# Memory sums joined with a U round, denominators from GpSimd sums, and a halved last tile, in a fused attention and SwiGLU kernel

## The chip, the cores and the metric

One core of one Trainium2 chip. The metric is the device time of one execution in microseconds (us), the median of several; lower is better. A profile is one further execution; its span is about 2 us shorter than the time on the device. Batch numbers run from 0 to 7, and "batch b" also names the part of the program in which batch b's gate and value matmuls run.

## The reference

Cut to what matters:

```python
a = exp(phi - max(phi)); a = a / (sum(a over the 32 memories) + 1e-9)      # (8, 8, 576, 32)
k_m = einsum('bhsm,bhsd->bhmd', a, k);  v_m = einsum('bhsm,bhsd->bhmd', a, v)
scores = q @ k_m.T / 8;  attn = softmax(scores);  x = attn @ v_m           # heads side by side: (4608, 512)
out = (silu(x @ w_gate) * (x @ w_val)) @ w_out                             # 512 -> 1536 -> 512
```

Inputs and output are float32. The kernel multiplies v_m into the two weight matrices first (the "U rounds"), so that gate and value come from the attention weights directly. It divides the memory sums by sums over the tokens ("denominators"), one for each head and memory.

## The kernel before

For each batch it makes memory sums (`kv_sum`: 48 matmuls, each on a strip of 32 array columns, four at a time), denominators (12 full-array matmuls with one moving column), a reciprocal and two normalisations on VectorE, and a transposition. Three U rounds (16 matmuls each, on tiles of 64 rows by 32 columns) and 24 "slots" follow. A slot is a gate pair, its silu on ScalarE, and the value pair and multiply of the slot before. Between the slots lie output matmuls of earlier batches. The whole is one hand-made order.

```python
def kv_denominators(b, p, o):
    for g in range(NG):
        for j in range(J):                                   # 2 x 6 matmuls
            nc.tensor.matmul(p[:, o + g:o + g + 1], lhsT=ephis[b][:, j, g]..., rhs=ones1[0:P, :], ...)
    r = att.tile([128, NG, 1, 1], FP32, tag="rS", name="t_rS")
    nc.vector.reciprocal(out=..., in_=p[:, o:o + NG])        # reads the denominators
# ...
def kv_items(b):
    def sums():
        box["kv"] = ps.tile([128, NG * 2 * D + NG], FP32, tag="b", name="p_kv")   # one PSUM tile for
        kv_sum(b, box["kv"], (0, 1))                                             # sums and denominators
    def norm():
        kv_denominators(b, box["kv"], o); k_norm(...); v_norm(...)
    return [lambda: (sums(), norm()), lambda: kv_T(b, (0, 1))]
# ... in the loop over batches, b = 2..7:
streams = [(g, 0, 24), (rest, 0, 24), ([u_item(b, 2)], 5, 6)]
streams += [([lambda: load_qT(b + 1)], n, n), (kv_items(b + 1), 8, 14),          # sums behind slot 9
            ([u_item(b + 1, 0)], 15, 17), ([u_item(b + 1, 1)], 21, 23)]
```

`spread` merges streams by their positions, counted in slots. PSUM is the memory that the matmuls write to; the pool `ps` has six of its banks, used in turn, and the output tiles have two more. SBUF is the memory that holds all other tiles.

The softmax here doesn't subtract the row's maximum and nothing guards it: scores larger than these inputs give would overflow.

Of the kernel before, what the change touches and what calls it, by code (L numbers as in the profile page):

```python
# [9 lines left out]
FP32 = mybir.dt.float32  # L10
BF16 = mybir.dt.bfloat16
# [3 lines left out]
def kernel(  # L15
# [17 lines left out]
    nc = tc.nc  # L33
    AF = mybir.ActivationFunctionType
    ALU = mybir.AluOpType

    B, H, S, D = q.shape
    M = phi.shape[3]
    DM, DF = moe_w_gate.shape
    P, J = 96, 6  # L40
    NG = 2
# [10 lines left out]
    att = ctx.enter_context(tc.tile_pool(name="att", bufs=2))  # L52
# [3 lines left out]
    ps = ctx.enter_context(tc.tile_pool(name="ps", bufs=6, space=bass.MemoryType.PSUM))  # L56
# [4 lines left out]
    out_r = out.rearrange("(b p j) c -> b j p c", b=B, p=P, j=J)  # L61
# [78 lines left out]
    ephis, rSs, bks, bvs, kTs, es, atts = {}, {}, {}, {}, {}, {}, {}  # L140

    def phi_exp(b):
        t = att.tile([P, J, NG, NP, M], BF16, tag="ephi", name="t_ephi")
        src = phis.pop(b).rearrange("p (i g) (j m) -> p g i j m", g=NG, m=M)
        for g in range(NG):
            nc.scalar.activation(  # L146
                out=t[:, :, g].rearrange("p j i m -> p i j m"), in_=src[:, g], func=AF.Exp
            )
        ephis[b] = t

    box = {}

    def kv_sum(b, p, parts):

        w0, w1 = parts[0], parts[-1] + 1
        n = (w1 - w0) * D
        for g in range(NG):
            for j in range(J):
                for i in range(NP):
                    nc.tensor.matmul(  # L160
                        p[32 * i:32 * i + 32, n * g:n * (g + 1)],
                        lhsT=ephis[b][:, j, g, i],
                        rhs=kvs[b][:, w0:w1, 2 * i + g, j * D:(j + 1) * D],
                        start=(j == 0),
                        stop=(j == J - 1),
                        tile_position=(0, 32 * i),
                    )

    def kv_denominators(b, p, o):
        for g in range(NG):  # L170
            for j in range(J):
                nc.tensor.matmul(  # L172
                    p[:, o + g:o + g + 1],
                    lhsT=ephis[b][:, j, g].rearrange("p i m -> p (i m)"),
                    rhs=ones1[0:P, :],
                    start=(j == 0),
                    stop=(j == J - 1),
                )
        r = att.tile([128, NG, 1, 1], FP32, tag="rS", name="t_rS")
        nc.vector.reciprocal(  # L180
            out=r.rearrange("p g a c -> p (g a c)"), in_=p[:, o:o + NG]
        )
        rSs[b] = r

    def k_norm(b, p):
        bk = att.tile([128, NG, 2, D], BF16, tag="bk", name="t_bk")
        nc.vector.tensor_tensor(
            out=bk,
            in0=p.to_broadcast([128, NG, 2, D]),
            in1=rSs[b].to_broadcast([128, NG, 2, D]),  # L190
            op=ALU.mult,
        )
        bks[b] = bk

    def v_norm(b, p):
        bv = att.tile([128, NG, D], BF16, tag="bv", name="t_bv")
        nc.vector.tensor_tensor(
            out=bv,
            in0=p,
            in1=rSs[b].rearrange("p g a c -> p g (a c)").to_broadcast([128, NG, D]),  # L200
            op=ALU.mult,
        )
        bvs[b] = bv

    def kv_T(b, parts):
        p = ps.tile([128, 3, 128], BF16, tag="b", name="p_T")
        if 0 in parts:
            kTs[b] = att.tile([128, 3, 128], BF16, tag="kT", name="t_kT")
        if 1 in parts:
            nc.tensor.transpose(p[:, 2], bvs.pop(b).rearrange("p g d -> p (g d)"), ident)  # L210
        if 0 in parts:
            bk = bks.pop(b)
            for g in range(NG):
                nc.tensor.transpose(p[:, g], bk[:, g].rearrange("p a d -> p (a d)"), ident)
        lo, hi = (0 if 0 in parts else 2), (3 if 1 in parts else 2)
        nc.vector.tensor_copy(out=kTs[b][:, lo:hi], in_=p[:, lo:hi])  # L216

    def kv_items(b):


        def sums():
            box["kv"] = ps.tile([128, NG * 2 * D + NG], FP32, tag="b", name="p_kv")
            kv_sum(b, box["kv"], (0, 1))

        def norm():
            o = NG * 2 * D
            kv_denominators(b, box["kv"], o)
            kvv = box["kv"][:, 0:o].rearrange("p (g w d) -> p g w d", g=NG, w=2)
            k_norm(b, kvv[:, :, 0:1, :])
            v_norm(b, kvv[:, :, 1, :])  # L230

        return [lambda: (sums(), norm()), lambda: kv_T(b, (0, 1))]

    def k_items(b):

# [118 lines left out]
    def flush_mul():  # L354
        while pend:
            pend.pop(0)()
# [44 lines left out]
    def token_segments(t0, count):  # L401
        segs = []
        t = t0
        while t < t0 + count:
            bb, rest = divmod(t, S)
            blk, pp = divmod(rest, P)
            n = min(P - pp, t0 + count - t)
            segs.append((t - t0, n, bb, 2 * (blk % 3) + blk // 3, pp))
            t += n
        return segs  # L410

    def out_units(c, u, eng):

        mine = {}

        def unit(jf):
            def run():
                if jf == 0:
                    mine["p"] = po.tile([128, DM], FP32, tag="o", name="p_oo")
                nc.tensor.matmul(  # L420
                    mine["p"],
                    lhsT=hts[c, jf][:, 128 * u:128 * (u + 1)],
                    rhs=WO[jf],
                    start=(jf == 0),
                    stop=(jf == NJF - 1),
                )
                if jf == NJF - 1:
                    t_o = work.tile([128, DM], FP32, tag="to", name="t_o")
                    if eng == "a":
                        nc.scalar.copy(out=t_o, in_=mine["p"])  # L430
                    else:
                        nc.vector.tensor_copy(out=t_o, in_=mine["p"])  # L432
                    for (r0, n, bb, jj, pp) in token_segments(2 * c * S + 128 * u, 128):
                        nc.sync.dma_start(
                            out=out_r[bb, jj, pp:pp + n, :], in_=t_o[r0:r0 + n, :]
                        )

            return run

        return [unit(jf) for jf in range(NJF)]  # L440

    def out_list(b):
        tiles = range(0, 4) if b % 2 == 0 else range(4, 9)
        res = []
        for n, u in enumerate(tiles):
            res += out_units(b // 2, u, "v" if n % 4 != 3 else "a")
        return res

    def q_items(b, evac):
# [4 lines left out]
    def u_item(b, c, evac="avav"):  # L454

        both = ((0, c, (0, 1)), (1, c, (0, 1)))
        return lambda: u_round(b, both, evac)
# [9 lines left out]
    def run(items):  # L467
        for x in items:
            x()
# [10 lines left out]
    def exp_tables():  # L480
        nc.scalar.preload_act_table_set("natural_log_exp_and_others")  # L481
# [108 lines left out]
    for b in range(2, B):  # L590
        last = b + 1 == B
        exp_tables()
        if b == 2:
            load_qT(2)
            phi_exp(2)
            run(take(28))
            run(kv_items(2)[:1] + take(6) + kv_items(2)[1:] + take(14))
        run(take(2))
        for g in range(NG):
            scores(b, g)  # L600
        if b + 2 < B:
            load_q(b + 2)
        if not last:
            load_k(b + 1)
            load_v(b + 1)
        if b + 2 < B:
            load_phi(b + 2, nc.gpsimd)
        run(take(8))
        if not last:
            phi_exp(b + 1)  # L610
        for g in range(NG):
            z_inv(b, g)
        nc.scalar.preload_act_table_set("silu_and_others")
        run(take(14))
        norm(b, 0)
        norm(b, 1)
        if b == 2:
            run(take(4))
            run([u_item(2, 0)] + take(6) + [u_item(2, 1)])
        run(take(12))  # L620
        rest = take(len(backlog))
        g = gv_slots(b)
        streams = [(g, 0, 24), (rest, 0, 24), ([u_item(b, 2)], 5, 6)]
        if not last:
            n = 12 if b == 2 else 0
            streams += [
                ([lambda: load_qT(b + 1)], n, n),
                (kv_items(b + 1), 8, 14),
                ([u_item(b + 1, 0)], 15, 17),
                ([u_item(b + 1, 1)], 21, 23),  # L630
            ]
        spread(*streams)
        flush_mul()
        backlog += out_list(b)
# [29 lines left out]
```

## Time and profile before

| | before |
|---|---|
| time, 6 runs in the same rounds as the change | 254.95 us (254.66 to 255.45) |
| span of the profiled run, mean granted TensorE clock | 252.3 us, 0.997 |
| busy: TensorE, VectorE, ScalarE, GpSimd | 243.2, 153.5, 167.0, 36.3 us |
| v of batch 3: issued, landed | 70.96, 87.9 us |
| batch 2: first gate matmul to the next scores | 80.79 to 100.00 us |

TensorE is the engine to watch: it never rests for long after the start, and its granted clock, the row below in tenths of full speed for 40 equal slices of the span, is low in no slice before the last.

```profile
PEclk9999999999999999999999999999999999999998
```

### The profile page before, as it was taken

How to read it: one execution, taken by the hardware profiler on the slowest of the kernel's cores; microseconds unless marked ns; L12 is line 12 of the kernel's file. 1: busy time of each engine (PE TensorE's matmuls, PEld its weight loads, DVE VectorE, ACT ScalarE, POOL GpSimd, SP SyncE). 2: the span in 40 equal slices, each digit the busy share in tenths (PEclk: the TensorE clock that was granted, in tenths of full speed). 3: DMA queues.
4: the chain of work that ended last, by engine and by line, in shares of the span. 5: the costliest groups of instructions: out<-in, count | busy, mean ns of one | idle time of the engine just before them, and what ended most of it. 6: DMA issues, size and time to landing. Idle time of an engine off the chain costs nothing.

```text
span 252.3 us, 6668 instructions
## 1 busy us (share of the span) xinstructions
PE 243.2 (96%) x2642; PEld 148.9 (59%) x2642; DVE 153.5 (61%) x334; ACT 167.0 (66%) x364; POOL 36.3 (14%) x53
## 2 busy tenths in 40 slices
PE   7999799999999999999999999999999999999992
PEld 7976467674544565467645665466645765467541
DVE  0027699993217878377927776487826775587321
ACT  2459689884095758965896578875896668676200
POOL 8433354000140004004000150000000000000000
PEclk9999999999999999999999999999999999999998
DMA  6999999999799998993994599990035211310143
GB/s 184 205 203 201 198 197 203 227 218 150 160 178 244 262 151 125 244 240 42 202 224 107 96 165 238 230 234 5 5 83 136 44 42 44 83 44 0 52 114 83
DMA packets 49006, 36.99 MB, mean 147 GB/s; under 512 B 15952, under 2 KB 43600, under 8 KB 48976
## 3 DMA queue, kind: packets, MB, share of 16 engines
q0 software_dynamic: 27632, 22.42, 55.8%
q1 hardware_dynamic: 20560, 13.57, 22.7%
q10 hardware_dynamic: 784, 0.59, 0.9%
q8 instruction: 20, 0.33, 0.5%
q14 instruction: 10, 0.08, 0.1%
HBM read 42.47 MB, written 9.44 MB: 206 GB/s over the span
## 4 chain that ended last, share of the span: by engine, by line
PE 68%; DMA 27%; POOL 1%; issue 1%; DVE 1%; ACT 0%; POOLq 0%; SPq 0%
PE p_oo L420 29%; PE p_g L364 15%; PE p_v L364 15%; DMA t_kv<-in_v_dram 13%; DMA t_q<-in_q_dram 12%; PE p_u L330 4%; DMA t_qT<-t_q 2%; PE p_kv L160 2%; PE p_kv L172 1%; PE p_g L287 1%; POOL t_kv L74 1%; PE p_v L307 1%; PE p_g L307 1%; POOL t_q L93 0%; POOL t_phi L69 0%
## 5 line engine op out<-in xcount | busy, mean ns | idle before, releaser
L420 PE MATMUL p_oo<-WO,t_h 128*128 128x512 bf16 x432 | 113.1, 379 | 0.0
L380 ACT ACTIVATE t_sg<-p_g 128x288 bf16<-128x288 f32 x192 | 77.2, 415 | 39.6 <-PE p_g L364 33.8
L387 DVE TENSOR_TENSOR t_h<-t_sg,p_v 128x288 bf16<-128x288 bf16 x192 | 84.3, 452 | 22.4 <-PE p_v L364 18.9
L364 PEld LDWEIGHTS <-t_U 128*128 128x128 bf16 x768 | 72.6, 98 | 35.6 <-issue 6.8
L364 PE MATMUL p_g<-t_A,t_U 128*128 128x288 bf16 x384 | 78.5, 286 | 0.8 <-ACT t_U L346 0.8
L364 PE MATMUL p_v<-t_A,t_U 128*128 128x288 bf16 x384 | 77.6, 286 | 0.0
L420 PEld LDWEIGHTS <-t_h 128*128 128x128 bf16 x432 | 41.5, 98 | 40.0 <-issue 2.8
L432 DVE COPY t_o<-p_oo 128x512 f32<-128x512 f32 x28 | 19.3, 691 | 47.2 <-PE p_oo L420 45.0
L348 DVE CAST t_U<-p_u 128x512 bf16<-128x512 f32 (+1 forms) x52 | 31.2, 642 | 1.0 <-PE p_u L330 0.5
L346 ACT CAST t_U<-p_u 128x512 bf16<-128x512 f32 (+1 forms) x52 | 26.2, 556 | 7.1 <-PE p_u L330 6.9
L93 POOL DMA_DIRECT2D t_q<-in_q_dram x6 | 4.6, 774 | 91.7 <-DMA t_qT<-t_q 90.9
L430 ACT COPY t_o<-p_oo 128x512 f32<-128x512 f32 x8 | 4.7, 591 | 19.7 <-PE p_oo L420 10.2
L490 PE MATMUL p_oo<-bones 128*128 128x128 bf16 x218 | 15.9, 234 | 1.5 <-DVE bones L502 1.5
L330 PE MATMUL p_u<-W,t_kT 64*32 64x512 bf16 (+1 forms) x416 | 15.7, 365 | 0.7 <-DVE t_kT L216 0.7
L490 PEld LDWEIGHTS <-bones 128*128 128x128 bf16 x218 | 14.2, 106 | 2.2 <-DVE bones L502 1.5
L146 ACT ACTIVATE t_ephi<-t_phi 96x768 bf16<-96x768 f32 x16 | 12.5, 844 | 4.2 <-DMA t_phi<-in_phi_dram 4.2
L180 DVE RECIPROCAL t_rS<-p_kv 128x2 f32<-128x2 f32 x8 | 1.4, 171 | 18.5 <-PE p_kv L172 18.5
L316 DVE TENSOR_TENSOR t_A<-t_E,t_lz 128x576 bf16<-128x576 bf16 x16 | 11.5, 750 | 0.4 <-ACT t_lz L311 0.4
L311 ACT ACTIVATE t_lz<-t_lz 128x576 f32<-128x576 f32 x16 | 10.9, 683 | 0.5
L481 ACT ACT_TABLE_LOAD x7 | 9.0, 1283 | 1.3 <-PEq L648 1.2
L330 PEld LDWEIGHTS <-t_kT 64*32 64x32 bf16 x416 | 4.3, 89 | 8.3 <-issue 6.6
L160 PE MATMUL p_kv<-t_kv,t_ephi 96*32 96x128 bf16 (+1 forms) x480 | 7.3, 210 | 0.7 <-DMA t_kv<-in_v_dram 0.7
(42 smaller groups left out, 127.8 us busy)
## 6 DMA issues: line engine op xcount, KB each, us to landing
t_kv<-in_k_dram POOLq DMA_DIRECT2D x8, 576.0 KB, 11.0
t_kv<-in_v_dram POOLq DMA_DIRECT2D x8, 576.0 KB, 16.4
out_dram<-t_o SPq DMA_DIRECT2D x24, 192.0 KB, 2.6
t_phi<-in_phi_dram POOLq DMA_DIRECT2D x6, 576.0 KB, 14.5
t_q<-in_q_dram POOLq DMA_DIRECT2D x6, 576.0 KB, 7.4
out_dram<-t_o SPq DMA_DIRECT2D x24, 128.0 KB, 2.4
W<-in_moe_w_gate_dram POOLq DMA_DIRECT2D x6, 256.0 KB, 13.1
W<-in_moe_w_val_dram POOLq DMA_DIRECT2D x6, 256.0 KB, 13.0
```

Source lines behind the costliest of these rows:

```text
L146: nc.scalar.activation(out=t[:, :, g].rearrange("p j i m -> p i j m"), in_=src[:, g], func=AF.Exp)
L160: nc.tensor.matmul(p[32 * i:32 * i + 32, n * g:n * (g + 1)], lhsT=ephis[b][:, j, g, i], rhs=kvs[b][:, w0:w1, 2 * i + g, j * D:(j + 1) * D] ...
L316: nc.vector.tensor_tensor(out=a, in0=es.pop((b, g)), in1=lzs.pop((b, g)), op=ALU.mult)
L330: nc.tensor.matmul(p[g][32 * i:32 * i + 32, f0:f1], lhsT=kTs[b][64 * g:64 * g + 64, 2, 32 * i:32 * i + 32], rhs=W[which, c][64 * g:64 * g ...
L346: nc.scalar.copy(out=t, in_=p)
L348: nc.vector.tensor_copy(out=t, in_=p)
L364: nc.tensor.matmul(p[:, 0:HALF], lhsT=Us[b, which, c, g][:, 128 * o:128 * (o + 1)], rhs=atts[b, g][:, r], start=(g == 0), stop=(g == NG - 1),)
L380: nc.scalar.activation(out=sg, in_=gate, func=AF.Silu)
L387: nc.vector.tensor_tensor(out=dst, in0=sg, in1=val, op=ALU.mult)
L420: nc.tensor.matmul(mine["p"], lhsT=hts[c, jf][:, 128 * u:128 * (u + 1)], rhs=WO[jf], start=(jf == 0), stop=(jf == NJF - 1),)
L432: nc.vector.tensor_copy(out=t_o, in_=mine["p"])
L490: nc.tensor.matmul(p[:, 0:128], lhsT=bones, rhs=bones, start=True, stop=True)
```

## The change

Its intent: fewer small matmuls and fewer changes of TensorE's tiling. GpSimd, nearly idle, adds the six token groups of exp(phi) and splits the sum into two bf16 terms, so 4 instead of 12 matmuls give the denominators. These stand first, then the sums, then a U round right behind them, as one stretch. The stretch has a new place, position 5 to 11 instead of 8 to 14. The very last output tile is copied in two halves by two engines and sent from two queues.

```diff
+    def phi_sum(b):
+        e = ephis[b].rearrange("p j g i m -> p j (g i m)")
+        t = att.tile([P, NG * 128], FP32, tag="es", bufs=1, name="t_es")
+        nc.gpsimd.tensor_tensor(out=t, in0=e[:, 0], in1=e[:, 1], op=ALU.add)
+        for j in range(2, J):
+            nc.gpsimd.tensor_tensor(out=t, in0=t, in1=e[:, j], op=ALU.add)
+        hl = att.tile([P, 2, NG * 128], BF16, tag="ehl", bufs=1, name="t_ehl")
+        nc.gpsimd.tensor_copy(out=hl[:, 0], in_=t)
+        nc.gpsimd.tensor_tensor(out=hl[:, 1], in0=t, in1=hl[:, 0], op=ALU.subtract)
...
+        def run_sums():
+            p = ps.tile([128, o + NG], FP32, tag="b", name="p_kv")
+            kv_denominators(b, p, o)          # ends with the reciprocal, as before
+            kv_sum(b, p, (0, 1))
             k_norm(...); v_norm(...)
+            if beside:
+                beside()                      # the U round
...
+                    if eng == "av":
+                        nc.scalar.copy(out=t_o[:, 0:h], in_=mine["p"][:, 0:h])
+                        nc.vector.tensor_copy(out=t_o[:, h:], in_=mine["p"][:, h:])
...
             phi_exp(b + 1)
+            phi_sum(b + 1)
...
-                (kv_items(b + 1), 8, 14),
+                (kv_items(b + 1, u_item(b, 2)), 5, 11),
```

More of the change, by code (lines that the diff above doesn't have):

```diff
@@ L151 @@
     box = {}
+    esums = {}
+    def phi_sum(b):
[7 more added lines that the diff above has]
+        nc.gpsimd.tensor_tensor(out=hl[:, 1], in0=t, in1=hl[:, 0], op=ALU.subtract)
+        esums[b] = hl
     def kv_sum(b, p, parts):
@@ L169, in kv_denominators, with kv_reciprocal @@
     def kv_denominators(b, p, o):
+        if b in esums:
+            hl = esums.pop(b)
+            terms = [[hl[:, t, 128 * g:128 * (g + 1)] for t in range(2)] for g in range(NG)]
+        else:
+            terms = [
+                [ephis[b][:, j, g].rearrange("p i m -> p (i m)") for j in range(J)]
+                for g in range(NG)
+            ]
         for g in range(NG):
-            for j in range(J):
+            for n, x in enumerate(terms[g]):
                 nc.tensor.matmul(
                     p[:, o + g:o + g + 1],
-                    lhsT=ephis[b][:, j, g].rearrange("p i m -> p (i m)"),
+                    lhsT=x,
                     rhs=ones1[0:P, :],
-                    start=(j == 0),
-                    stop=(j == J - 1),
-                )
+                    start=(n == 0),
+                    stop=(n == len(terms[g]) - 1),
+                )
+        kv_reciprocal(b, p, o)
+    def kv_reciprocal(b, p, o):
         r = att.tile([128, NG, 1, 1], FP32, tag="rS", name="t_rS")
@@ L216, in kv_T, with kv_items @@
         nc.vector.tensor_copy(out=kTs[b][:, lo:hi], in_=p[:, lo:hi])
-    def kv_items(b):
-        def sums():
-            box["kv"] = ps.tile([128, NG * 2 * D + NG], FP32, tag="b", name="p_kv")
-            kv_sum(b, box["kv"], (0, 1))
-        def norm():
+    def kv_items(b, beside=None):
+        def run_sums():
             o = NG * 2 * D
-            kv_denominators(b, box["kv"], o)
-            kvv = box["kv"][:, 0:o].rearrange("p (g w d) -> p g w d", g=NG, w=2)
+            p = ps.tile([128, o + NG], FP32, tag="b", name="p_kv")
+            kv_denominators(b, p, o)
+            kv_sum(b, p, (0, 1))
+            kvv = p[:, 0:o].rearrange("p (g w d) -> p g w d", g=NG, w=2)
             k_norm(b, kvv[:, :, 0:1, :])
             v_norm(b, kvv[:, :, 1, :])
-        return [lambda: (sums(), norm()), lambda: kv_T(b, (0, 1))]
+            if beside:
+                beside()
+        return [run_sums, lambda: kv_T(b, (0, 1))]
     def k_items(b):
@@ L428, in run @@
                     t_o = work.tile([128, DM], FP32, tag="to", name="t_o")
-                    if eng == "a":
+                    if eng == "av":
+                        h = DM // 2
+                        nc.scalar.copy(out=t_o[:, 0:h], in_=mine["p"][:, 0:h])
+                        nc.vector.tensor_copy(out=t_o[:, h:], in_=mine["p"][:, h:])
+                    elif eng == "a":
                         nc.scalar.copy(out=t_o, in_=mine["p"])
@@ L433, in run @@
                     for (r0, n, bb, jj, pp) in token_segments(2 * c * S + 128 * u, 128):
-                        nc.sync.dma_start(
-                            out=out_r[bb, jj, pp:pp + n, :], in_=t_o[r0:r0 + n, :]
-                        )
+                        o_r = out_r[bb, jj, pp:pp + n, :]
+                        if eng == "av":
+                            nc.scalar.dma_start(out=o_r[:, 0:h], in_=t_o[r0:r0 + n, 0:h])
+                            nc.sync.dma_start(out=o_r[:, h:], in_=t_o[r0:r0 + n, h:])
+                        else:
+                            nc.sync.dma_start(out=o_r, in_=t_o[r0:r0 + n, :])
             return run
@@ L445, in out_list @@
         for n, u in enumerate(tiles):
-            res += out_units(b // 2, u, "v" if n % 4 != 3 else "a")
+            eng = "av" if b + 1 == B and u == tiles[-1] else "v" if n % 4 != 3 else "a"
+            res += out_units(b // 2, u, eng)
         return res
@@ L622 @@
         g = gv_slots(b)
-        streams = [(g, 0, 24), (rest, 0, 24), ([u_item(b, 2)], 5, 6)]
+        streams = [(g, 0, 24), (rest, 0, 24)]
+        if last:
+            streams += [([u_item(b, 2)], 5, 6)]
         if not last:
```

## The prediction

> **What bounds the kernel now.** I read the busy shares first, then the chain that ended last, then the timeline of TensorE around one memory sum and one U round, then the waits of TensorE, and the timeline of VectorE before the gate and value rounds.
>
> ```profile
> PE 243.2 (96%) x2642; PEld 148.9 (59%) x2642; DVE 153.5 (61%) x334; ACT 167.0 (66%) x364; POOL 36.3 (14%) x53
> ...
> PE 68%; DMA 27%; POOL 1%; issue 1%; DVE 1%; ACT 0%; POOLq 0%; SPq 0%
> ```
>
> TensorE is busy nearly throughout, and the chain is TensorE work plus 27% DMA. The chain in order of time says where the DMA part lies: before about 88 us. From there to the end it is TensorE, without a break. So after 88 us, time saved on TensorE is time saved, and every stall of TensorE is paid in full; before 88 us loads set the pace. The last load on the chain is v of batch 3:
>
> ```profile
> 69.44 0.67 POOL t_q L93
> 70.20 0.76 POOL t_kv L74
> 70.96 16.95 DMA t_kv<-in_v_dram
> 88.05 0.85 PE p_kv L160 x48
> 88.91 0.39 PE p_kv L172 x12
> ```
>
> The reader is to see that v of batch 3 lands at 70.96 + 16.95 = 87.9 us and that its memory sums start right then. TensorE's timeline of that place (start, length, what) and of a quiet one later:
>
> ```profile
> 83.88 0.41 PE L364 MATMUL p_v<-t_A,t_U 128*128 128x288 bf16 x2
> 84.22 0.63 PE L330 MATMUL p_u<-W,t_kT 64*32 64x512 bf16 x16
> 84.78 0.39 PE L420 MATMUL p_oo<-WO,t_h 128*128 128x512 bf16 x1
> ...
> 87.15 0.41 PE L364 MATMUL p_v<-t_A,t_U 128*128 128x288 bf16 x2
> 88.05 0.85 PE L160 MATMUL p_kv<-t_kv,t_ephi 96*32 96x128 bf16 x48 [0.49 <-DMA t_kv<-in_v_dram]
> ...
> 114.36 0.41 PE L364 MATMUL p_v<-t_A,t_U 128*128 128x288 bf16 x2
> 114.70 0.85 PE L160 MATMUL p_kv<-t_kv,t_ephi 96*32 96x128 bf16 x48
> 115.48 0.45 PE L172 MATMUL p_kv<-ones,t_ephi 96*128 96x1 bf16 x12
> 115.80 0.41 PE L364 MATMUL p_g<-t_A,t_U 128*128 128x288 bf16 x2
> ```
>
> A pair of gate or value matmuls starts every 0.245 us (288 columns each). After the pair at 83.88 the next instruction could start at 84.13; the U round starts at 84.22 and the next full-array matmul at 84.78. A U round therefore costs 0.65 us: single starts in the trace give 0.10 to get in, 0.44 of work (two waves of eight), 0.12 to get out. Memory sums with denominators cost 115.80 - 114.60 = 1.19 us: 0.10 in, 0.68 of sums, 0.10 out, 0.31 for twelve one-column matmuls at about 25 ns.
>
> **What the Trainium skill says.** "TensorEngine Tiling (Array Packing)", Key Properties: a change of tiling mode, not just of tile, drains TensorE. The trace agrees: the 0.10 and 0.12 us on either side of each column-tiled stretch. Sums (96 rows by 32 columns) and U (64 by 32) are by that page's list two modes, so joining them need not make their border free.
> "GPSIMD Engine Reference", section 3.1: an add of two fp32 tensors with 2048 columns took 4497 ns on GpSimd. No run here has such an add yet; scaled to 256 columns plus some dispatch I estimate 0.6 us each.
> "SBUF — State Buffer", Who interferes with whom: a VectorE instruction with two SBUF inputs contends with a GpSimd instruction that reads SBUF, and the later one waits for the whole earlier one. In this kernel only the softmax normalisation (t_A from t_E and t_lz) has two SBUF inputs; before has nothing on GpSimd to meet it, so its trace cannot say.
> "TensorE: Matmul & The Clock Gate", Part 1: an idle window of about 3.4 us halves the clock. Before has no such gap after the start, and its granted clock is 1.00 in every stretch from 62 to 235 us.
>
> **The change, part by part.**
> Denominators, batches 3 to 7: 8 of 12 one-column matmuls go, 8 x 25 ns = 0.20 us each batch. GpSimd gets seven operations per batch, about 4.2 us by the estimate above, in a time in which it is idle.
> Joined stretch, same batches: before 1.19 + 0.65 = 1.84 us. After: four denominators 0.11, in 0.10, sums 0.68, border x, U 0.44, out 0.12 = 1.45 + x. The whole gain is 0.39 - x; with x about 0.1, as for the other mode changes, 0.3 us per batch.
> Moved: the order of TensorE's instructions shows that the sums now stand after gate slot 6 instead of slot 9, three slots earlier, with U2 behind them. In batches 3 to 6 the loads allow it: v of batch 4 is issued at 96.27 and lands 11.3 us later, at 107.6, while the new place is near 111.5. So four batches gain 4 x 0.3 = 1.2 us.
> In batch 2 (sums of batch 3) the load does not allow it. Up to the end of slot 5 nothing changes (84.13 us). Then come one output matmul (0.22), slot 6 (0.49) and the denominators (0.11): TensorE arrives at 84.95 and v lands at 87.9 as before, since nothing ahead of it in the queues changes. It stands about 3.0 us, where before stood 0.5. At 88.05 the new kernel has yet to do what the old had done: U2, slots 7 to 9 (3 x 0.49 = 1.47) and two output matmuls (0.43; order counts four before the stretch where before had six). From there to slot 10 the old kernel needs sums and denominators, 1.09; the new one needs sums 0.68, border 0.1, U 0.44, out 0.12, then 1.47 + 0.43 = 3.24. Loss in batch 2: 2.1 us, its own joining gain already inside.
> Last tile: the copy that ends the kernel is
>
> ```profile
> 247.91 0.69 DVE L432 COPY t_o<-p_oo 128x512 f32<-128x512 f32 x1 [4.49 <-PE p_oo L420]
> ```
>
> Half of it by VectorE takes some 0.42 us (its 256-column casts of U took 417 ns), the ScalarE half about the same (375 ns), side by side. The two transfers of each half are issued from two queues, two per queue as before. Gain 0.27 us.
>
> Sum without contention: 254.82 + 2.1 - 1.2 - 0.3 = 255.4. I add 0.1 for PSUM: the joined stretch takes five of six banks at once, and VectorE must do two normalisations (0.3 and 0.2 us between starts) before its two casts (0.6 each); by my count the banks come free within 0.1 us of when the next slots want them.
>
> **Rivals.**
> GpSimd against the normalisation. In batch 3:
>
> ```profile
> 102.12 1.58 ACT L146 ACTIVATE t_ephi<-t_phi 96x768 bf16<-96x768 f32 x2
> ...
> 106.42 1.42 DVE L316 TENSOR_TENSOR t_A<-t_E,t_lz 128x576 bf16<-128x576 bf16 x2
> ```
>
> GpSimd may start once the exponentials end at 103.7 and works to about 108; VectorE's two normalisations at 106.42 to 107.84 fall inside, and the gate round that reads them starts at 108.21. With up to 0.6 us of waiting before each, they end 0.3 to 1.2 us later, of which about 0.4 is slack: 0 to 0.8 us of stall in each of batches 3 to 6, so 0 to 3 us. For it: the skill and the timing. Against it: it has not been seen here, and if the sums take under 0.4 us each GpSimd is done first. In batch 2 two U rounds lie between, so there is slack. I count 0.4 us for it, a sixth of the worst. If it is whole, the time is about 258.
> The stall cools TensorE. Three us of standing is just short of the 3.4 us window; if it counts, several us at half clock follow and cost 1.5 to 2 us more, 257.5. I give it one in ten.
> The load lands earlier, or the stretch waits for nothing. Then batch 2 gains 0.3 like the others instead of losing 2.1, and the time is 253.2. Against it: before already waited 0.49 us for this very transfer at a place 3 us later. I give it one in eight.
> The border costs nothing (x = 0): 0.5 us better.
> GpSimd as a queue. It also issues the loads, and now cannot run ahead of its sums: k and v of batch 7, issued at 147 us before, must wait for the exponentials of batch 6, about 160. They are needed at 195 and take 10 to 19 us: hidden.
>
> **Range and chances.** 255.4 + 0.1 + 0.4 = 255.9. Eight in ten between 253.8 (v early, or x = 0 with no contention) and 258.3 (full contention, or a cold clock). Two per cent is 5.1 us: no single rival reaches it, and slower needs contention and cooling together. Faster by 2% would need 249.7, more than all savings together.
>
> **What would show it.** Right: a wait of TensorE for v of about 3 us at the first joined stretch, near 85 us, and none at the four later ones; those four stretches, from denominators to the next full-array matmul, at about 1.55 us. GpSimd's sums at 4 us per batch. The normalisations longer or later than 106.4 plus 1.42 would show contention, and then an idle of TensorE before the first gate matmul of the batch. A granted clock under 1.00 after 88 us would show cooling. The last copy at 0.4 us in two engines. Wrong: v landing before 86 us, or TensorE waiting at the stretch for GpSimd's sums instead.

## The result, and the profile after

261.54 us (259.99 to 263.70, 6 runs) against 254.95 us: slower. The ratio is 1.0259, 95% interval 1.0209 to 1.0308. Here and below a ratio is the mean time of one kernel's fast runs over that of the other's fast runs of the same rounds, so it is not quite the ratio of the medians. All six runs count as fast runs, yet their mean granted clocks lie between 0.983 and 0.993. The output is correct.

The busy row and the clock row of the changed kernel's page, and the first row of its chain:

```profile
PE 243.0 (93%) x2575; PEld 150.7 (58%) x2602; DVE 155.9 (60%) x334; ACT 167.5 (64%) x365; POOL 62.4 (24%) x88
...
PEclk9999999999999779999999999999999999999998
...
PE 81%; DMA 8%; DVE 5%; ACT 2%; issue 2%; POOL 0%; DVEq 0%
```

By the page TensorE is busy about as long as before (27 of its 2602 matmuls are missing from this record), so most of the lost 7.9 us of span is not more work. Two slices near 90 us show a low clock, and VectorE, 1% of the chain before, is now 5%. Starts of single instructions give where the time came from. Each row runs from a batch's first gate matmul to the next batch's first score matmul; what lies between these rows takes the same in both kernels, within 0.01 us.

| part | before, us | after, us | difference |
|---|---|---|---|
| start to the first scores of batch 2 | 69.10 | 69.44 | +0.35 |
| batch 2 | 19.21 | 24.56 | +5.35 |
| batch 3 | 18.22 | 18.80 | +0.58 |
| batch 4 | 20.81 | 21.34 | +0.53 |
| batch 5 | 18.22 | 18.61 | +0.39 |
| batch 6 | 20.81 | 21.33 | +0.52 |
| batch 7, to the last matmul's start | 27.75 | 27.75 | 0.00 |
| last matmul's start to the end | 4.84 | 5.02 | +0.19 |

The sum is 7.9 us. Batch 2, the load and the clock: TensorE's timeline, then busy times and clock by stretch (the columns are the stretch and its length; the busy times of TensorE, its weight loads, VectorE, ScalarE and GpSimd, with counts; the clock; the share of DMA and its GB/s).

```profile
85.18 0.24 PE L193 MATMUL p_kv<-ones,t_ehl 96*128 96x1 bf16 x4
88.98 1.47 PE L173 MATMUL p_kv<-t_kv,t_ephi 96*32 96x128 bf16 x48 [3.56 <-DMA t_kv<-in_v_dram]
90.38 1.05 PE L354 MATMUL p_u<-W,t_kT 64*32 64x512 bf16 x16
91.37 0.66 PE L388 MATMUL p_g<-t_A,t_U 128*128 128x288 bf16 x2
```

```profile
84.36:87.77 3.41, 1.07 (x12) 0.73 (x9) 1.34 (x4) 0.82 (x2) 0.00 (x0) 1.00 1.21 281
87.77:91.18 3.41, 2.20 (x64) 1.38 (x64) 0.68 (x3) 0.10 (x1) 0.00 (x0) 0.50 1.15 237
91.18:94.60 3.42, 3.20 (x19) 1.80 (x13) 2.12 (x4) 1.71 (x4) 0.00 (x0) 0.50 0.36 80
94.60:98.01 3.41, 3.41 (x29) 2.62 (x28) 2.26 (x6) 2.21 (x6) 3.09 (x4) 1.00 0.54 52
```

TensorE reaches the stretch at 85.2 and stands until v lands at 88.8. The clock halves at 87.77, while it stands, and is back at 94.60: the sums take 1.40 us to the start of the U round, against 0.78 in every other batch. When the clock steps is seen again under experiment 8.

The later batches: TensorE and VectorE at the joined stretch of batch 4.

```profile
146.32 0.24 PE L193 MATMUL p_kv<-ones,t_ehl 96*128 96x1 bf16 x4
146.96 0.85 PE L173 MATMUL p_kv<-t_kv,t_ephi 96*32 96x128 bf16 x48 [0.40 <-DVE t_rS L204]
147.74 0.63 PE L354 MATMUL p_u<-W,t_kT 64*32 64x512 bf16 x16
148.30 0.42 PE L388 MATMUL p_g<-t_A,t_U 128*128 128x288 bf16 x2
```

```profile
146.37 0.45 DVE L411 TENSOR_TENSOR t_h<-t_sg,p_v 128x288 bf16<-128x288 bf16 x1 [0.25 <-PE p_v L388]
146.75 0.16 DVE L204 RECIPROCAL t_rS<-p_kv 128x2 f32<-128x2 f32 x1
```

This was in none of my steps. The sums wait for the reciprocal, and the reciprocal waits its turn on VectorE behind the multiply of the slot before. Sums and denominators share a PSUM tile; VectorE reads the denominators from it and TensorE then writes the sums to it, and a semaphore holds the sums until the read is over. From first denominator to first sum it takes 0.64 us in batches 4 and 6 and 0.86 in 3 and 5. The joined stretch takes 148.30 - 146.32 = 1.98 us, where sums, denominators and U round took 1.84 apart.

The normalisations of batch 4 on VectorE and, beside them, GpSimd:

```profile
139.46 2.24 DVE L340 TENSOR_TENSOR t_A<-t_E,t_lz 128x576 bf16<-128x576 bf16 x2
```

```profile
137.04 0.66 POOL L158 TENSOR_TENSOR t_es<-t_ephi 96x256 f32<-96x256 bf16 x1 [10.99 <-ACT t_ephi L146]
137.78 3.30 POOL L160 TENSOR_TENSOR t_es<-t_es,t_ephi 96x256 f32<-96x256 f32 x4
141.14 0.81 POOL L162 CAST t_ehl<-t_es 96x256 bf16<-96x256 f32 x1
```

The pair takes 2.24 us where it took 1.42 before, and GpSimd's sums lie around it. The second gate matmul of the batch comes late, 0.51 us after the first instead of 0.12. The end of the kernel, ScalarE and VectorE:

```profile
255.63 0.37 ACT L455 COPY t_o<-p_oo 128x256 f32<-128x256 f32 x1 [2.00 <-DMA out_dram<-t_o]
```

```profile
256.03 0.42 DVE L456 COPY t_o<-p_oo 128x256 f32<-128x256 f32 x1 [4.89 <-ACT t_o L455]
```

The halves do not run side by side: a semaphore holds VectorE until ScalarE has ended, and 0.37 + 0.42 is more than the 0.69 of one copy. The halves share the PSUM tile that they read and the SBUF tile that they write; which of the two the semaphore guards no run separates.

### The profile page after: what moved, and what is told of

Same layout as the page of the kernel before. It is cut to its first block, busy times and chain, and to the rows that moved or that the text cites. A ratio compares the mean times of both kernels' runs of the same rounds, so it can differ in the third digit from the quotient of the medians.

```text
span 260.2 us, 6617 instructions
## 1 busy us (share of the span) xinstructions
PE 243.0 (93%) x2575; PEld 150.7 (58%) x2602; DVE 155.9 (60%) x334; ACT 167.5 (64%) x365; POOL 62.4 (24%) x88
## 4 chain that ended last, share of the span: by engine, by line
PE 81%; DMA 8%; DVE 5%; ACT 2%; issue 2%; POOL 0%; DVEq 0%
PE p_oo L444 27%; PE p_g L388 20%; PE p_v L388 18%; DMA t_kv<-in_v_dram 7%; PE p_u L354 5%; PE p_oo L522 5%; PE p_kv L173 3%; DVE t_A L340 1%; PE p_g L311 1%; DVE t_h L411 1%; DMA out_dram<-t_o 1%; PE p_g L331 1%; DVE t_o L460 1%; PE p_v L331 1%; ACT L593 0%
## 5 line engine op out<-in xcount | busy, mean ns | idle before, releaser
L444 PE MATMUL p_oo<-WO,t_h 128*128 128x512 bf16 x405 | 106.3, 380 | 0.9 <-issue 0.3
L388 PE MATMUL p_g<-t_A,t_U 128*128 128x288 bf16 x384 | 79.7, 289 | 2.6 <-ACT t_U L370 1.0
L460 DVE COPY t_o<-p_oo 128x512 f32<-128x512 f32 x27 | 18.6, 688 | 40.3 <-PE p_oo L444 40.1
L158 POOL TENSOR_TENSOR t_es<-t_ephi 96x256 f32<-96x256 bf16 x5 | 3.3, 663 | 55.3 <-ACT t_ephi L146 55.3
L160 POOL TENSOR_TENSOR t_es<-t_es,t_ephi 96x256 f32<-96x256 f32 x20 | 14.9, 747 | 1.6
L340 DVE TENSOR_TENSOR t_A<-t_E,t_lz 128x576 bf16<-128x576 bf16 x16 | 14.8, 953 | 0.4 <-ACT t_lz L335 0.4
L173 PE MATMUL p_kv<-t_kv,t_ephi 96*32 96x128 bf16 (+1 forms) x480 | 8.0, 219 | 5.8 <-DMA t_kv<-in_v_dram 3.6
L173 PEld LDWEIGHTS <-t_ephi 96*32 96x32 bf16 x480 | 6.9, 101 | 6.9 <-issue 6.5
```

The lines of the kernel that those rows point to most:

```text
L160: nc.gpsimd.tensor_tensor(out=t, in0=t, in1=e[:, j], op=ALU.add)
L173: nc.tensor.matmul(p[32 * i:32 * i + 32, n * g:n * (g + 1)], lhsT=ephis[b][:, j, g, i], rhs=kvs[b][:, w0:w1, 2 * i + g, j * D:(j + 1) * D] ...
L340: nc.vector.tensor_tensor(out=a, in0=es.pop((b, g)), in1=lzs.pop((b, g)), op=ALU.mult)
L388: nc.tensor.matmul(p[:, 0:HALF], lhsT=Us[b, which, c, g][:, 128 * o:128 * (o + 1)], rhs=atts[b, g][:, r], start=(g == 0), stop=(g == NG - 1),)
L444: nc.tensor.matmul(mine["p"], lhsT=hts[c, jf][:, 128 * u:128 * (u + 1)], rhs=WO[jf], start=(jf == 0), stop=(jf == NJF - 1),)
L460: nc.vector.tensor_copy(out=t_o, in_=mine["p"])
```

## The experiments

Ten kernels ran, all with correct results. The first four shared one chip, the next four a second, the last two a third. Each was compared with runs of the kernel before on its own chip, so ratios are compared across the groups, not times. The change itself was not run again beside them; where intervals overlap, the trace has to decide.

**1. The reciprocal behind the sums.**

```diff
             kv_denominators(b, p, o)      # without its reciprocal
             kv_sum(b, p, (0, 1))
+            kv_reciprocal(b, p, o)
```

> The changed kernel with the reciprocal of the denominators issued behind the memory sums instead of ahead of them. Theory (sums and denominators share one PSUM tile, so the sums wait until VectorE has read the denominators, and VectorE comes to that only after its queued multiply): the waits of the sums for the reciprocal (2.3 us in all, 0.4 to 0.65 in each later batch) are gone, batches 3 to 6 lose nothing or gain 0.1 to 0.3 us each, and the time falls from 261.5 by 2.2 to 2.6 us, to about 259.0. Rival (the wait only moves: VectorE's later normalisations hold the five PSUM banks and the next slots wait for those): the waits appear at the gate or value matmuls behind the stretch and the time falls by under 1 us. The first stretch keeps its wait for v and its cold clock under both.

Measured: 259.75 us (258.79 to 261.10, 4 runs), ratio 1.0176 (1.0121 to 1.0231) against the change's 1.0259 (1.0209 to 1.0308). The difference of 0.0083 is 2.1 us of 255; the two intervals overlap, so the size rests on the trace. There, no wait for the reciprocal is left. TensorE at batch 4:

```profile
146.45 0.24 PE L193 MATMUL p_kv<-ones,t_ehl 96*128 96x1 bf16 x4
146.62 0.85 PE L173 MATMUL p_kv<-t_kv,t_ephi 96*32 96x128 bf16 x48
147.41 0.62 PE L355 MATMUL p_u<-W,t_kT 64*32 64x512 bf16 x16
147.96 0.42 PE L389 MATMUL p_g<-t_A,t_U 128*128 128x288 bf16 x2
148.41 0.42 PE L389 MATMUL p_v<-t_A,t_U 128*128 128x288 bf16 x2
```

First denominator to first sum is now 0.17 us in each of batches 3 to 6, where it was 0.86, 0.64, 0.86 and 0.64: 2.3 us saved. The joined stretch takes 147.96 - 146.45 = 1.52 us, 0.33 less than the 1.84 apart, as foreseen. The rival is partly right too. The value pair starts at 148.41, 0.45 us after the gate pair instead of 0.245: by the order of the pool it takes the bank of the sums, and it starts 0.06 us after VectorE has read that bank for the last time (148.35). That gives back 0.2 us in batch 4. Batches 3 to 6 differ from before by -0.03, +0.26, -0.22 and +0.26 us: that none of them would lose was a miss, since the late normalisations, experiment 4, are still in.

**2. The first joined stretch back at its old place.**

```diff
-                (kv_items(b + 1, u_item(b, 2)), 5, 11),
+                (kv_items(b + 1, u_item(b, 2)), *((8, 14) if b == 2 else (5, 11))),
```

> The changed kernel with the joined stretch of batch 2 alone back at its old place (after gate slot 9), all else as changed. Theory (the early place costs the wait for v and, through it, the clock): the granted clock is 1.00 throughout after the start, the wait for v shrinks to under 1 us, and the time falls from 261.5 by 4.5 to 5.3 us, to about 256.5. Rival (only the wait counts; the low clock is a coincidence or a run in another state): a low clock is seen near 90 us even so, and the time falls by 2.1 to 2.7 us, to about 259.

Measured: 257.27 us (256.75 to 257.66, 4 runs), ratio 1.0074; 1.0259 - 1.0074 is 4.7 us. The clock rows show 1.00 from 62 to 235 us. At the head of the list of TensorE's waits stands this (what waited for what, us in all, times, longest):

```profile
PE p_kv L173 <- DVE t_rS L204: 3.0, 6, 0.7
```

Of the wait for v at most the 0.7 us at the first joined stretch are left: reciprocal and v both arrive at 88.45, and the sums start at 88.59.

So the three slots by which one stretch moved are two thirds of the change's loss, and the rival's 2.1 to 2.7 us falls.

**3. Dummy matmuls in the wait.**

```diff
             kv_denominators(b, p, o)
+            if b == 3:
+                warm(50)
             kv_sum(b, p, (0, 1))
```

> The changed kernel with 50 dummy matmuls of 128 columns (some 2.8 us) between denominators and sums of the first joined stretch, in the time in which TensorE stands and waits for v. Theory (standing idle for 3.6 us is what halves the clock, and that costs 2.7 us beyond the wait): the sums still start when v lands, near 88.9 us, the granted clock stays 1.00, the sums take 0.78 instead of 1.40 us, and the time falls by about 2.7 us to 258.8. Rival (the low clock comes from elsewhere): sums at 1.40 us again and no gain.

Measured: 259.60 us (259.43 to 260.31, 4 runs), ratio 1.0171 (1.0130 to 1.0212); 1.0259 - 1.0171 is 2.2 us. TensorE:

```profile
85.93 0.24 PE L193 MATMUL p_kv<-ones,t_ehl 96*128 96x1 bf16 x4
86.04 2.95 PE L524 MATMUL p_oo<-bones 128*128 128x128 bf16 x50
88.92 0.85 PE L173 MATMUL p_kv<-t_kv,t_ephi 96*32 96x128 bf16 x48
89.70 0.62 PE L356 MATMUL p_u<-W,t_kT 64*32 64x512 bf16 x16
```

The sums start no earlier (88.92 against 88.98), but at full speed. (v had landed at 88.57; the dummies held them some 0.3 us longer.) From there to the next U round takes 7.10 us (to 96.02) against 9.72 (to 98.70): the half clock costs 2.6 us. Standing idle causes it, since work of no use prevents it: the mean clock was 0.995 or more in all four runs, 0.993 or less in all six of the change.

**4. GpSimd's sums alone, added to the kernel before, their result unused** (the edit is `phi_sum` and its call).

> The kernel before plus the GpSimd sums alone, their result unused. Theory (GpSimd reading SBUF and the normalisation with two SBUF inputs take turns): the normalisations take 0.9 to 1.2 us instead of 0.75 in batches 3 to 6, the second gate matmul of these batches comes 0.2 us late and a further 0.0 to 0.2 is lost, together 0.8 to 1.1 us: 255.9. Rival (the sums cost nothing by themselves; what is lost in these batches comes from the joined stretch): 254.9 and normalisations at 0.75 us.

Measured: 257.33 us (255.78 to 259.31, 4 runs), ratio 1.0081. In the profile batches 3 to 6 are longer than before by 0.22, 0.39, 0.04 and 0.39 us, 1.04 in all, and this with the old stretches. VectorE and TensorE at batch 4:

```profile
137.46 2.24 DVE L329 TENSOR_TENSOR t_A<-t_E,t_lz 128x576 bf16<-128x576 bf16 x2
```

```profile
139.24 0.29 PE L377 MATMUL p_g<-t_A,t_U 128*128 128x288 bf16 x1
139.76 0.28 PE L377 MATMUL p_g<-t_A,t_U 128*128 128x288 bf16 x1 [0.23 <-DVE t_A L329]
```

The second gate matmul comes 0.52 us after the first instead of 0.12. In batches 3 to 6 it is late by 0.23, 0.39, 0.04 and 0.40 us, as much as each batch is longer. That settles where these 1.04 us come from. What I had not expected was batch 2: v landed at 90.5 us, TensorE waited 3.0 us at the old place, and the clock was halved here as well.

**5. The same, without the sums that run while v of batch 3 is under way.**

> The kernel before plus the unused GpSimd sums for batches 4 to 7 only; batch 3's, which run while v of batch 3 is on its way, are left out. Theory A (in the run with all sums, v of batch 3 landed at 90.5 us instead of 88.0 because GpSimd's sums held up that load): v lands near 88 again, the clock stays 1.00, and only the 1.0 us of the normalisations in batches 3 to 6 remains: ratio 1.004 to before. Theory B (v's landing varies by itself, as two of seven runs of before with a mean clock of 0.991 suggest): v's landing and the clock scatter as with all sums, ratio 1.004 to 1.010.

Measured: 256.96 us (255.33 to 260.25, 4 runs), ratio 1.0052 with an interval of 0.9987 to 1.0118. In the profiled run v landed at 88.0 us and batches 3 to 6 were 0.97 us longer, but two of the four runs had mean clocks of 0.989 and 0.991. So the slow clock comes without those sums, and theory A is not needed. In the twelve traces v takes 17.0 to 19.8 us from issue to landing: 17.0 in the trace of before; 17.9 and 19.1 in experiments 7 and 8 below, which have no GpSimd sums at all. Whether the sums add something to that scatter stays open.

**6. The same sums, held back until the batch's second normalisation is done.**

```diff
         norm(b, 1)
+        if not last:
...
+            nc.gpsimd.tensor_copy(out=gate, in_=atts[b, 1][0:P, 0, 0:2])   # makes GpSimd wait
+            phi_sum(b + 1)
```

> The kernel before plus all unused GpSimd sums, each batch's started only when the second normalisation of the batch is done (a two-column copy of its result on GpSimd holds them back). Theory (GpSimd and the normalisation take turns at reading SBUF): normalisations at 0.75 us, no late second gate matmul, batches 3 to 6 as long as in the kernel before (18.22 and 20.81 us from first gate matmul to next scores). Rival (GpSimd slows other VectorE work too, multiplies or casts): these batches stay 0.1 us or more too long. The time is 254.9 to 257 by how v of batch 3 lands.

Measured: 254.64 us (254.08 to 257.24, 6 runs), ratio 0.9979 (0.9951 to 1.0006): no cost of the sums can be told from noise. VectorE's normalisations and GpSimd's cast at batch 4:

```profile
135.21 1.42 DVE L329 TENSOR_TENSOR t_A<-t_E,t_lz 128x576 bf16<-128x576 bf16 x2
```

```profile
140.53 0.39 POOL L162 CAST t_ehl<-t_es 96x256 bf16<-96x256 f32 x1
```

The pair takes 1.42 us again, batches 3 to 6 are as long as before to the hundredth (18.22, 20.81, 18.22 and 20.81 us), and GpSimd gains as well: its cast takes 0.39 us where it took 0.81 against the normalisation. It is the meeting of these two that costs, not GpSimd's work as such.

**7. The halved last tile alone, and 8. the last tile as two PSUM tiles of 256 columns**, one after the other, each copied by VectorE and sent from its own queue.

```diff
+                for jf in (2 * (k % 6), 2 * (k % 6) + 1):          # 8: six such units for each half
+                    nc.tensor.matmul(mine["p"][:, 0:hw], lhsT=..., rhs=WO[jf][:, hw * x:hw * (x + 1)], ...)
+                if k % 6 == 5:
+                    nc.vector.tensor_copy(out=t_o, in_=mine["p"][:, 0:hw])
```

> The kernel before plus the last output tile in two halves as in the change. Theory (both halves read one PSUM tile and write one SBUF tile, and VectorE's half waits for ScalarE's): from the start of the last matmul to the end of the span 0.1 to 0.3 us more than the 4.8 us of the kernel before; the VectorE half starts when the ScalarE half ends. Rival (the longer tail of the changed kernel came with the rest of the change): the halves side by side and 0.27 us less.

> The kernel before with the last output tile computed as two PSUM tiles of 256 columns, one after the other (24 matmuls of 256 instead of 12 of 512), each copied by VectorE and sent from its own queue. Theory: the first half is copied and sent while the second is computed, the last copy takes 0.42 instead of 0.69 us and waits for nothing, and the stretch from the last matmul's start to the end is 0.3 to 0.4 us shorter than in the kernel before (0.1 of it because the last matmul is half as long); TensorE's part is no longer. Rival (weight loads for twice the matmuls show): the last tile's matmuls take over 0.2 us more and eat it.

One run each, for the trace only: 255.15 and 257.56 us. In 7 the last matmul's start to the end is 4.90 us against 4.84 before, and VectorE's half starts 0.03 us after ScalarE's ends. The stretch scatters: the six traces with a whole tile have 4.72 to 4.84 us, the five with the halved one 4.80 to 5.11, by their means 0.2 us more. So the split gives nothing and costs about 0.2 us, as the 0.19 of the table. In 8 that stretch is 4.71 us; but the smaller matmuls end later, and from the last value matmul's start to the end both are equal (17.70 before, 17.71 here). The last copy did shrink to 0.42 us, but the second of its two transfers took 0.85 us to issue instead of 0.41. My theory for 8 missed. The run of 8 is slow as that of experiment 4 was, by a late v (89.62 us), though up to its last tile it is the kernel before. It holds the shortest wait that went with a halved clock; below it, two stretches of this run and two of experiment 6, whose wait of 1.78 us left the clock at 1.00:

```profile
89.75 1.21 PE L160 MATMUL p_kv<-t_kv,t_ephi 96*32 96x128 bf16 x48 [2.35 <-DMA t_kv<-in_v_dram]
```

```profile
86.67:90.08 3.41, 1.06 (x30) 0.65 (x31) 0.91 (x2) 0.64 (x2) 0.00 (x0) 1.00 1.18 275
90.08:93.49 3.41, 3.41 (x60) 2.28 (x49) 1.25 (x4) 0.60 (x2) 0.00 (x0) 0.50 0.97 138
```

```profile
85.83:89.24 3.41, 2.47 (x19) 1.58 (x17) 2.60 (x6) 2.11 (x6) 0.00 (x0) 1.00 1.19 280
89.24:92.65 3.41, 2.57 (x72) 2.13 (x73) 1.16 (x5) 0.73 (x2) 0.00 (x0) 1.00 1.25 228
```

The length of the wait alone does not decide. In the clock records of these traces every step lies a whole number of 3.413 us after the first rise: in the change the rise is at 5.85, the fall at 87.77 (24 times 3.413 later), the return at 94.60 (26 times); in 8 they are at 4.75, 90.08 (25) and 93.49 (26).

The clock fell, in the change and in 1, 4 and 8, after a stretch of this grid in which TensorE had stood 2.3 to 3.1 of the 3.41 us; it stayed where TensorE stood 1.2 us or less, and the 1.78 us of experiment 6 are split by the grid into 0.94 and 0.84. Where between 1.2 and 2.3 us the limit lies is not shown. It came back after the first stretch in which TensorE worked nearly throughout. In 4 and 8 that was the next one, and batch 2 lost 1.5 us beside its longer wait; in the change and in 1, v landed in the middle of the next one, and the low clock lasted two.

**9. The kernel before with the sums of batch 3 at slot 13.**

```diff
-                (kv_items(b + 1), 8, 14),
+                (kv_items(b + 1), *((12, 16) if b == 2 else (8, 14))),
```

> The kernel before with one change: the memory sums of batch 3 stand three slots later (about slot 13 instead of 9), where v of batch 3 has landed even in the late cases seen (87.9 to 90.5 us). Theory (how long TensorE waits for this one load decides both the 0.5 us wait and, in some runs, the halved clock of the kernel before): no wait for v, 0.5 us less than before's usual run, 254.4, and none of its runs above 255.5 with a mean clock near 0.991. Rival (the slow runs have another cause): as much scatter as before.

Measured: 253.91 us (253.63 to 254.39, 6 runs) against 255.11 (253.90 to 258.41, 11 runs, two of them with clocks of 0.991 and 0.993); ratio of fast runs 0.9964 (0.9941 to 0.9988). The wait of this stretch is gone: the sums start at 89.37, v landed at 88.54. The fast runs range over 0.8 us, those of before over 1.8. None of these six runs was slow, where two of eleven were; that is too few to show that the slow runs are gone, and a v as late as in experiment 4 (90.5) would still be waited for. That the kernel before stands on the same edge is shown by experiment 8; the change stepped over it.

**10. The change mended**: joined stretch and GpSimd denominators, with the edits of 1, 6 and 9, the other stretches at their old place, the last tile as before.

> The change mended: stretch joined and denominators from GpSimd as in the change, but the reciprocal behind the sums, the GpSimd sums started only after the batch's second normalisation, the sums of batch 3 at slot 13 and of the others at the old slot 9, the last tile as before. Theory: each of five joined stretches takes 1.52 us instead of 1.85 in two parts, of which 0.1 to 0.2 us is given back where a value matmul waits for the bank of the sums, so 0.15 to 0.25 us each, about 1.0 us in all, besides the 0.5 us of the later place: 253.4, ahead of before and of the later place alone. Rival (what is saved at the stretch comes back behind it in full): no better than the later place alone, 254.4.

Measured: 253.56 us (253.18 to 253.91, 6 runs), ratio 0.9951 (0.9927 to 0.9976). TensorE at batch 4:

```profile
141.30 0.24 PE L193 MATMUL p_kv<-ones,t_ehl 96*128 96x1 bf16 x4
...
142.82 0.42 PE L389 MATMUL p_g<-t_A,t_U 128*128 128x288 bf16 x2
143.27 0.42 PE L389 MATMUL p_v<-t_A,t_U 128*128 128x288 bf16 x2
```

Batches 3 to 6 take 18.09, 20.69, 18.09 and 20.69 us, 0.12 less than before each. The stretch saves 0.33; the value pair at 143.27 comes 0.45 us after the gate pair instead of 0.245, as in experiment 1, and gives 0.2 of it back. The expected 0.15 to 0.25 us was a little too much. It has the lowest median, but its lead over experiment 9 (0.35 us) rests on the trace: the two intervals overlap.

## Why the prediction was wrong

It foresaw 255.9 us, within 2%, and measured were 261.5. Two steps failed: the sum for the joined stretch left out a wait, and the chance of cooling was far too low. By its own steps:

- **The bound, and that the loads of batch 2 do not allow the move: right.** TensorE stood at the first joined stretch and at no other for a load. The size was off by 0.6 us (3.6 instead of 3.0 us of wait), because I took v's landing, 87.9 us, from the one trace there was; of the twelve traces it is the one with the quickest landing, not a usual one. The loss foreseen without cooling, 2.1 us, is what experiment 3 measures, where the dummies fill a gap of 3.0 us: batch 2 takes 21.14 us, 1.93 more than before.
- **"The stall cools TensorE", one in ten and 1.5 to 2 us: the mechanism was right, the chance was not.** All six runs had a mean clock of 0.993 or less; experiment 3 measures the half clock at 2.6 us. I compared a wait of 3.0 us with a window of 3.4 us and called it just short; a wait of 2.35 us was enough (experiment 8), because the clock fell after a stretch in which TensorE had stood for most of the 3.41 us, not for all. My cost fits one such stretch (1.5 us in experiments 4 and 8); the profiled run of the change had two. This is the largest term.
- **"After: four denominators 0.11, in 0.10, sums 0.68": the step that failed outright.** It counts TensorE's own work and asks for no wait inside the stretch. With the denominators and their reciprocal ahead of the sums in one PSUM tile, the sums wait for VectorE: 0.64 to 0.86 us instead of 0.17 (experiment 1), 2.3 us in batches 3 to 6. The four gains of 0.3 us became a loss. The order that I read shows the denominators moving ahead, and not one of my rivals asked who reads that tile.
- **The joining itself, 0.39 - x with x near 0.1: right.** Without the wait the stretch took 1.52 us instead of 1.84. Sums to U round took 0.78 us, as sums to denominators had, so the border between the two tilings costs as much as the others.
- **GpSimd against the normalisation: right in mechanism and range** (0 to 3 us foreseen, 1.04 measured alone in experiment 4, counted at 0.4). TensorE idles before the second gate matmul of a batch, not before the first. The seven operations took 4.8 us undisturbed (experiment 6) and 5.7 in the change, not 4.
- **GpSimd as a queue: right.** k and v of batch 7 were issued at 171.8 and 172.6 us (foreseen about 160) and v landed at 182.9; batch 7 is as long as before.
- **PSUM, 0.1 us:** hidden in the change behind its other waits; 0.2 us in batch 4 once those are gone (experiments 1 and 10).
- **Last tile, 0.27 us gained:** I took "side by side" for granted. The halves run one after the other, and about 0.2 us are lost (experiment 7).
- **"Slower needs contention and cooling together": wrong.** Both came, but without the 1.0 us of contention the time would still be about 260.5 us, 2.2% above 254.95; cooling and the wait for the reciprocal, which I did not have, are enough.

Of the 7.9 us of span, batch 2's 5.35 are the predicted 2.1, 0.6 of later load and 2.6 of half clock. Batches 3 to 6 are -1.3 of joining, +2.3 of reciprocal and +1.0 of normalisation, 2.0 together, as in the table. The last tile has 0.19, and 0.35 lie ahead of batch 2, which no experiment separates from the scatter of the first loads (first scores between 68.9 and 70.2 us in the twelve traces).

## What to carry to other kernels

Before moving work earlier, ask for each operand when it lands, in more than one run: an engine that sits half a microsecond behind a load stands on an edge, and the price of stepping over it is the wait plus a slow clock. A short instruction whose result another engine reads is not free in the middle of a stretch, if the stretch then writes to the same tile: put the reader behind the last writer, or give it another tile. An idle engine's work is not free by itself: GpSimd's sums made the normalisations wait, and the cost (1.0 us here) was gone when their start was moved.

## What the Trainium skill lacked or had wrong

- "TensorE: Matmul & The Clock Gate", Why this matters for your kernels: it warns of gaps of more than about 3 us between matmuls. Here less was enough: with a wait of 2.35 us (experiment 8; 2.3 of a stretch of 3.41 us stood idle) the granted clock fell to 0.50, while one of 1.78 us, split by the grid of stretches, left it at 1.00. In the change the half clock lasted from 87.8 to 94.6 us and cost 2.6 us.
- "TensorEngine Tiling (Array Packing)", Key Properties: it says that a change of mode drains TensorE, without a duration. Here 0.10 us into and 0.10 to 0.12 us out of a column-tiled stretch, and about 0.1 us between two column-tiled modes (sums to U round 0.78 us, sums to full array 0.79).
- "SBUF — State Buffer", Who interferes with whom: it agrees. Two normalisations with two SBUF inputs took 2.24 us instead of 1.42 beside GpSimd's adds, and on GpSimd a delayed add took 1.07 us instead of 0.66 and a cast 0.81 instead of 0.39.
- "GPSIMD Engine Reference", section 3.1: its 2048-column figure, scaled, gave my estimate of 0.6 us for an add of 256 columns; 0.66 us was measured, so the page served.
- No page read tells how much the landing of one load scatters from run to run: 17.0 to 19.8 us from issue for the same transfer in twelve traces of twelve kernels.
